# Normalised tiles transposed on TensorE instead of by DMA, with one PSUM bank set aside for it

## The chip, the cores and the metric

The kernel runs on one core of one Trainium2 chip. The metric is device time in microseconds (us) of one execution, all inputs in device memory at the start. The kernel before takes 1333.68 us (median of three runs, 1333.62 to 1335.79). In what follows PE is the matrix engine TensorE, PEld its weight loads, DVE is VectorE, ACT ScalarE, POOL GpSimd, and SP the engine that issues most of the DMAs. PSUM is the small memory that TensorE writes its results to, here eight banks of 128 x 512 fp32; SBUF is the large on-chip memory that everything else reads.

## What is computed

Two kinds of layer, each applied twice in turn to x (2048 positions, 1024 channels, bf16). Cut to what matters:

```
def _A_ref(x, wqkv, wo):          # attention, 32 heads of 32, window of 8 positions, 2 apart
    q, k, v = split(x @ wqkv)
    idx = pos[:, None] - arange(8)[None, :] * 2      # masked where negative
    attn = softmax(einsum("bhsd,bhswd->bhsw", q, k[idx]) * scale)
    return einsum("bhsw,bhswd->bhsd", attn, v[idx]) @ wo

def _B_ref(x, w1, b1, w2, b2):    # MLP over positions: S=2048 -> F=3584 -> S=2048
    u = gelu(einsum("bsd,sf->bdf", layernorm(x), w1) + b1)
    return (einsum("bdf,fs->bds", u, w2) + b2).transpose

x = x + A(layernorm(x));  x = x + B(layernorm(x))
x = x + A(layernorm(x));  x = x + B(layernorm(x))
```

## The kernel before

**Tiling.** Positions are taken in two classes, even (c = 0) and odd (c = 1), since the attention window steps by two; each class is 8 tiles of 128 positions by 1024 channels. A layer pair (`li` = 0, 1) is attention, then the MLP.

**hT.** The projections of attention need the normalised input with channels on the partitions, so each 128 x 1024 tile must be transposed after its layer norm. `hT[c][hf]` holds a class in two halves of 512 positions (four tiles each). For the first class of the first layer `first_tiles` does this on TensorE (`turn`, L278 to L281: eight 128 x 128 transposes into a PSUM bank; `place`, L284: one copy to hT). All the others, 24 tiles, go through `to_hT` (L231, L232): one transposing DMA from SP's queue. They are

- the second class of layer 0, normalised in `prologue_tile` (L334): 8 tiles early in the kernel; odd tiles are normalised on ACT, even ones on DVE;
- the first class of layer 1: `gemm2_tile` (L638) computes a tile of the MLP's second product (56 matmuls into two banks), adds bias and residual on DVE (L654), normalises into `hb` (DVE), and hands it to `to_hT`: 8 tiles one after another between the layers;
- the second class of layer 1, again `gemm2_tile`, normalised on ACT for six of eight tiles: 8 tiles, mixed into attention as fill.

**Attention.** `project` (L389) takes one output tile and one half: 8 matmuls (L400) into one bank, copied by ACT to q, k or v (L404, L407). `qk` (L422) multiplies q and shifted k on DVE (T, L430) and sums over channels on TensorE (L435). Softmax runs on DVE and ACT, its result goes to device memory and comes back spread over partitions (`pb`, L472); `pv` multiplies and adds on DVE (L490, L501, L503). `out_proj` (L560, matmuls L590) closes the layer. `gemm1` (L613, matmuls L623) is the first product of the MLP.

**Order.** `weave` (L685) walks the steps of attention (the lead) and, where its own running estimate of TensorE and DVE time says that the next TensorE step would wait, pulls a unit of fill: in this order second-class tiles, v projections of the second class (`v_ahead`), and, once `out0` is opened, output projection of the first class and partial sums of the MLP. In that estimate the step that ends a tile of the second class counts 0.6 us of TensorE time. This sets the order in which the instructions are traced. The order on each engine is then fixed when the program is built, by priorities in order of tracing; only the opening (`first_tiles`) is pinned by hand on PE, DVE, ACT and POOL. `proj_pair` (L410) has a special order for the pair that opens a class: k and q of the first half of the positions, then of the second half, so that the first 32 matmuls need only tiles 0 to 3. For c = 0 it serves layer 1 alone, since layer 0 opens with `first_tiles`.

**Queues and banks.** SP's queue carries every weight load (L378 wq and wv, L567 wo, L610 w1, L677 w2) and, between them, the transposing DMAs of L232; POOL's queue carries activations (xs, xr, xa, xb) and the softmax traffic. PSUM: the pool `psp` has 6 banks, shared by everything that TensorE accumulates, and `pssp` holds the scores in 2.

Of the kernel before, what the change touches and what calls it, by code (L numbers as in the profile page):

```python
# [13 lines left out]
BF16 = mybir.dt.bfloat16  # L14

P = 128
# [10 lines left out]
def kernel(  # L27
# [13 lines left out]
    nc = tc.nc  # L41
# [4 lines left out]
    KD = D // P  # L46
# [24 lines left out]
    def pool(name, bufs, **kw):  # L71
        return ctx.enter_context(tc.tile_pool(name=name, bufs=bufs, **kw))
# [9 lines left out]
    pbp = pool("pbp", 2)  # L82
    otp = pool("otp", KD)
    dram = pool("dram", 1, space=bass.MemoryType.DRAM)
    psp = pool("psp", 6, space=bass.MemoryType.PSUM)
    pssp = pool("pssp", 1, space=bass.MemoryType.PSUM)

    class at:
# [15 lines left out]
    def bank(name="ps"):  # L104
        return psp.tile([P, 512], FP32, name=name, tag="ps")

    def x2(name, shape=None, dt=BF16):
        return x2p.tile(shape or [P, D], dt, name=name, tag="x2")
# [14 lines left out]
    ident = const.tile([P, P], BF16, name="ident")  # L123
# [70 lines left out]
    def stats_dve(x, mul, eps):  # L194

        s = st("bn", [P, D // 512, 6])
        for cc in range(D // 512):
            nc.vector.bn_stats(out=s[:, cc, :], in_=x[:, cc * 512:(cc + 1) * 512])
        mv = st("mv", [P, 2])
        nc.vector.bn_aggr(out=mv[:], in_=s[:])  # L200
        rs = st("rs", [P, 1])
        rsqrt(rs[:], mv[:, 1:2], mul, eps)
        return mv[:, 0:1], rs

    def stats_act(x, mul, eps, junk, sums=None):

        s1 = sums
        if s1 is None:
            s1 = st("s1", [P, NDC])
            for n in range(NDC):  # L210
                nc.scalar.activation(out=junk[:, n * 512:(n + 1) * 512], in_=x[:, n * 512:(n + 1) * 512],
                                     func=ACT.Identity, accum_out=s1[:, n:n + 1])
        t1 = st("t1", [P, 1])
        nm = st("nm", [P, 1])
        nc.scalar.activation(out=t1[:], in_=s1[:, 1:2], func=ACT.Copy, scale=-1.0 / D)
        nc.scalar.activation(out=nm[:], in_=s1[:, 0:1], func=ACT.Identity, bias=t1[:], scale=-1.0 / D)
        ss = st("ss", [P, 1])
        nc.scalar.activation(out=junk, in_=x, func=ACT.Square, bias=nm[:], accum_out=ss[:])  # L218
        rs = st("rs", [P, 1])
        rsqrt(rs[:], ss[:], mul / D, eps)  # L220
        return nm, rs

    def norm_dve(dst, x, mean, rs, op=ALU.subtract):
        nc.vector.tensor_scalar(out=dst, in0=x, scalar1=mean, scalar2=rs[:], op0=op, op1=ALU.mult)

    def norm_act(dst, x, nm, rs):
        bi = st("bi", [P, 1])
        nc.scalar.activation(out=bi[:], in_=nm[:], func=ACT.Identity, scale=rs[:])
        nc.scalar.activation(out=dst, in_=x, func=ACT.Identity, bias=bi[:], scale=rs[:])  # L229

    def to_hT(h, hT, c, i):  # L231
        nc.sync.dma_start_transpose(out=hT[c][i // 4][:, :, (i % 4) * P:(i % 4 + 1) * P], in_=h)  # L232

    def staged(c, i):
        n = (i + c * (NT - 1)) % NT
# [98 lines left out]
    def prologue_tile(c, i, hT):  # L334
        t = staged(c, i)
        if i % 2:
            junk = x2("junk")
            nm, rs = stats_act(t, 1.0, eps1, junk[:])
            norm_act(t, t, nm, rs)
        else:  # L340
            mean, rs = stats_dve(t, 1.0, eps1)
            norm_dve(t, t, mean, rs)
        to_hT(t, hT, c, i)
# [5 lines left out]
    class Attn:  # L349
# [58 lines left out]
                               in_=ps[:].unsqueeze(1).to_broadcast([P, 2, HT]))  # L408

        def proj_pair(self, c, pair, parts):  # L410
            if pair == 0 and 0 in parts:
                for hf in range(2):
                    for part in parts:
                        for dt in range(2):
                            yield from self.proj(c, part, dt, hf)
                return
            for part in parts:
                for hf in range(2):
                    for dt in (2 * pair, 2 * pair + 1):
                        yield from self.proj(c, part, dt, hf)  # L420
# [217 lines left out]
    def gemm2_tile(c, i, w2t, src, dst, hT, on_act=False, end=False):  # L638
        xs = x2("xs")
        nc.gpsimd.dma_start(out=xs[:], in_=src[c][i * P:(i + 1) * P, :])  # L640
        xo = x2("xo")
        halves = [slice(n * 512, (n + 1) * 512) for n in range(NDC)]
        groups = [halves[:1], [slice(512, 768)], [slice(768, 1024)]] if end else [halves]
        for cols in groups:
            acc = [bank() for _ in cols]
            for n in range(NW2):
                for ft in range(n * HF, (n + 1) * HF):
                    for ps, xc in zip(acc, cols):
                        nc.tensor.matmul(ps[:, 0:xc.stop - xc.start], lhsT=w2t[n][:, ft % HF, c::DIL],  # L649
                                         rhs=g[ft // GF][:, ft % GF, xc], start=(ft == 0), stop=(ft == FT - 1))  # L650
                if n < NW2 - 1:
                    yield 1.5 * len(cols), 0.0
            for ps, xc in zip(acc, cols):
                nc.vector.scalar_tensor_tensor(out=xo[:, xc], in0=ps[:, 0:xc.stop - xc.start], scalar=b2_sb[:, i, c:c + 1],  # L654
                                               in1=xs[:, xc], op0=ALU.add, op1=ALU.add)
            yield 1.5 * len(cols), 0.75 * len(cols)
            if end:
                nc.sync.dma_start(out=dst[:, cols[0]], in_=xo[:, cols[0]])
        if not end:
            nc.gpsimd.dma_start(out=dst, in_=xo[:])  # L660
        if hT is None:
            return
        hb = x2("hb")
        if on_act:
            nm, rs = stats_act(xo[:], 1.0, eps1, hb[:])
            norm_act(hb[:], xo[:], nm, rs)
        else:
            mean, rs = stats_dve(xo[:], 1.0, eps1)
            norm_dve(hb[:], xo[:], mean, rs)
        to_hT(hb[:], hT, c, i)  # L670
        yield 0.6, 0.0 if on_act else 2.0

    def w2_tiles(i):
# [72 lines left out]
    hT = [[None, None] for _ in range(DIL)]  # L746
    new_hT(hT, 0)
    for li in range(2):
# [15 lines left out]
        def second_class():  # L764
            new_hT(hT, 1)
            for i in range(NT):
                if first:
                    prologue_tile(1, i, hT)
                    yield 0.6, 2.0 * (i % 2 == 0)
                else:  # L770
                    yield from gemm2_tile(1, i, w2_tiles(i), xa[0], xb[1][i * P:(i + 1) * P, :], hT, on_act=i < NT - 2)
# [20 lines left out]
        if first:  # L792
            with at(top):
                ln_exp_table()
            hT = [[None, None] for _ in range(DIL)]
            new_hT(hT, 0)
            for i in range(NT):
                run(gemm2_tile(0, i, w2_tiles(i), xa[0], xb[0][i * P:(i + 1) * P, :], hT))
        else:
            for i in range(NT):  # L800
                w2t = w2_tiles(i)
                for c in range(DIL):
                    run(gemm2_tile(c, i, w2t, xa[1], out_v[c, i], None, end=(i == NT - 1 and c == DIL - 1)))
# [30 lines left out]
```

## Time and profile before

| what | value |
|---|---|
| median of three runs | 1333.68 us |
| the profiled execution, its own time | 1335.79 us |
| its span, first to last instruction | 1334.0 us |
| granted TensorE clock, mean | 0.992 |
| PE busy, first product of the MLP (L623) | 386.2 us |
| PE busy, second product of the MLP (L649) | 388.6 us |
| transposing DMAs (L232) | 24, landing 3.0 / 4.1 / 12.3 us after issue (min / median / max) |
| 256-byte packets (those of the transposes) in the DMA record | 24,576, 6.29 MB |

How to read it: busy is the time in which an engine had an instruction running. A matmul of 512 columns is shown as 379 ns long, but the next one starts 216 ns after it: 56 matmuls of a `gemm2_tile` take 12.1 us. Idle time that the profile lists before an instruction is followed by what ended it ("<-DMA w" is a weight load that landed). SP is shown by what it issues: the start of a line is the moment at which SP got to that DMA, after waiting for its data or its buffer, and everything behind it in the queue waits too.

The stretches of the kernel: 0 to 33 us opening; 33 to about 260 attention of layer 0 with fill; to 490 the rest of the output projection and the MLP's first product; 488 to 585 the eight `gemm2_tile`s of the first class; 585 to about 910 attention of layer 1, into which the second class's eight are mixed (up to 777); then the MLP of layer 1 to the end.

### The profile page before, as it was taken

Reading aid. Unit: us, or ns where it says so; the run is one execution under the profiler, and the core shown is the slowest. Engines: PE = TensorE matmul, PEld = TensorE weight load, DVE = VectorE, ACT = ScalarE, POOL = GpSimd, SP = SyncE. Lnnn points to the kernel's source line nnn. Section 1 sums busy time; section 2 is a strip of 40 time slices with the busy share of each in tenths; the row PEclk is TensorE's granted clock in tenths of the full one; section 3 lists DMA queues with packets and bytes.
Section 4 is the critical chain, followed back from the end, with each engine's and each line's share of the span. In section 5 each row is a group of like instructions: output and inputs, shape, how many; then the busy total and the mean of one; then the engine's idle time right before and its main releaser. Section 6 shows DMA issues by size and latency. Waiting matters only on the chain. (4 is left out here: it accounts for less than half of the span.)

```text
span 1334.0 us, 15448 instructions
## 1 busy us (share of the span) xinstructions
PE 1285.8 (96%) x6226; PEld 582.9 (44%) x6348; DVE 658.4 (49%) x785; ACT 456.8 (34%) x808; POOL 95.5 (7%) x230
## 2 busy tenths in 40 slices
PE   8997999998999999999999999999999999999999
PEld 5343443343444444444444444444444444444444
DVE  6669597969401322325693149957981033110111
ACT  6844445931222430022524425477313234000000
POOL 3000001100100000000001110011020000000000
PEclk9998999998999999999999999999999999999999
DMA  9652525462522238873748962616444232334331
GB/s 258 138 134 63 135 81 144 159 162 71 173 63 79 77 105 222 212 179 90 179 118 219 252 163 64 157 65 179 129 123 122 63 95 71 117 89 142 117 115 61
DMA packets 239448, 173.00 MB, mean 130 GB/s; under 512 B 32208, under 2 KB 227152, under 8 KB 237328
## 3 DMA queue, kind: packets, MB, share of 16 engines
q1 hardware_dynamic: 224432, 116.67, 32.8%
q0 software_dynamic: 14368, 54.29, 14.7%
q8 instruction: 49, 0.80, 0.2%
q10 hardware_dynamic: 576, 1.05, 0.2%
q14 instruction: 23, 0.19, 0.0%
HBM read 146.81 MB, written 18.87 MB: 124 GB/s over the span
## 5 line engine op out<-in xcount | busy, mean ns | idle before, releaser
L649 PE MATMUL ps<-g,w 128*128 128x512 bf16 (+1 forms) x1781 | 388.6, 377 | 6.9 <-DMA w<-in_B_w_dram 4.8
L623 PE MATMUL ps<-h,w 128*128 128x512 bf16 x1757 | 386.2, 379 | 4.4 <-ACT h L229 2.3
L649 PEld LDWEIGHTS <-w 128*128 128x128 bf16 x1820 | 177.7, 98 | 217.3 <-DMA w<-in_B_w_dram 5.8
L623 PEld LDWEIGHTS <-w 128*128 128x128 bf16 x1792 | 175.3, 98 | 214.6 <-issue 3.6
L400 PE MATMUL ps<-hT,wq 128*128 128x512 bf16 (+1 forms) x1150 | 257.5, 376 | 5.2 <-issue 2.5
L654 DVE SCALAR_TENSOR_TENSOR xo<-ps,b_sb,xs 128x512 bf16<-128x512 f32 (+1 forms) x65 | 45.6, 738 | 296.7 <-PE ps L649 265.2
L430 DVE TENSOR_TENSOR T<-q,k 128x4096 bf16<-128x4096 bf16 x64 | 143.2, 2285 | 72.8 <-ACT q L404 52.7
L400 PEld LDWEIGHTS <-wq 128*128 128x128 bf16 x1176 | 114.4, 100 | 142.6 <-issue 17.5
L634 DVE TENSOR_TENSOR tmp<-ps,g 128x512 f32<-128x512 f32 x80 | 55.3, 692 | 213.6 <-PE ps L623 209.4
L501 DVE TENSOR_TENSOR pr<-pr 128x2048 bf16<-128x2048 bf16 x120 | 112.9, 947 | 0.6
L590 PE MATMUL ps<-wo,oT 128*128 128x512 bf16 x373 | 94.4, 383 | 8.6 <-DVE oT L503 6.8
L407 ACT CAST k<-ps 128x1024 bf16<-128x1024 f32 x64 | 64.6, 1014 | 86.9 <-PE ps L400 74.8
L490 DVE TENSOR_TENSOR pr<-pb,g 128x2048 bf16<-128x2048 bf16 x64 | 77.0, 1217 | 27.5 <-DMA pb<-pd 26.1
L400 PE MATMUL ps<-hT,wv 128*128 128x512 bf16 x376 | 87.6, 384 | 0.6 <-issue 0.2
L635 ACT ACTIVATE g<-tmp,b_sb 128x512 bf16<-128x512 f32 x80 | 57.7, 721 | 82.1 <-DVE tmp L634 82.1
L490 DVE TENSOR_TENSOR pr<-pb,v 128x2048 bf16<-128x2048 bf16 x64 | 76.3, 1215 | 10.7 <-DMA pb<-pd 9.8
L629 ACT CAST g<-ps 128x512 bf16<-128x512 f32 x80 | 45.7, 587 | 69.5 <-PE ps L623 69.2
L191 ACT ACTIVATE ln<-mv,eps 128x1 f32<-128x1 f32 x37 | 10.9, 294 | 166.7 <-DVE mv L200 159.5
L590 PEld LDWEIGHTS <-oT 128*128 128x128 bf16 x384 | 37.5, 99 | 56.3 <-DVE oT L503 7.8
L400 PEld LDWEIGHTS <-wv 128*128 128x128 bf16 x384 | 42.7, 114 | 43.1 <-issue 7.0
L435 PE MATMUL sc<-T,sel 128*32 128x512 bf16 x512 | 38.9, 387 | 15.2 <-DVE T L430 14.9
L404 ACT CAST q<-ps 128x512 bf16<-128x512 f32 x64 | 37.0, 584 | 48.0 <-PE ps L400 47.7
(97 smaller groups left out, 643.3 us busy)
## 6 DMA issues: line engine op xcount, KB each, us to landing
w<-in_B_w_dram SPq DMA_DIRECT2D x96, 448.0 KB, 3.8
w<-in_B_w_dram SPq DMA_DIRECT2D x56, 512.0 KB, 4.9
wq<-in_A_wqkv_dram SPq DMA_DIRECT2D x40, 512.0 KB, 4.3
pb<-pd POOLq DMA_DIRECT2D x16, 1024.0 KB, 10.7
wo<-in_A_wo_dram SPq DMA_DIRECT2D x16, 512.0 KB, 3.9
xa<-xn POOLq DMA_DIRECT2D x32, 256.0 KB, 3.2
xs<-xa POOLq DMA_DIRECT2D x32, 256.0 KB, 3.5
wv<-in_A_wqkv_dram SPq DMA_DIRECT2D x12, 512.0 KB, 5.0
```

The costliest lines, as they stand in the source:

```text
L400: nc.tensor.matmul(ps[:, lo:hi], lhsT=cols, rhs=self.hT[c][hf][:, kt, lo:hi], start=(kt == 0), stop=(kt == KD - 1))
L407: nc.scalar.copy(out=window(buf, 0, PADK + hf * HT, [(KW + 1, 2), (1, HT)]), in_=ps[:].unsqueeze(1).to_broadcast([P, 2, HT]))
L430: nc.vector.tensor_tensor(out=T[:], in0=q[:].unsqueeze(1).to_broadcast([P, 4, SC]), in1=window(k, par, 2, [(2, 4), (1, SC)]), op=ALU.mult)
L490: nc.vector.tensor_tensor(out=pr[:, :, u, :], in0=pb[:, :, u, :], in1=window(v, par, 2 + hf * HT, [(TB, 4), (2, 4), (1, TB)]), op=ALU.mult)
L501: nc.vector.tensor_tensor(out=pr[:, :, 0:wd, :], in0=pr[:, :, 0:wd, :], in1=pr[:, :, wd:2 * wd, :], op=ALU.add)
L590: nc.tensor.matmul(ps[:], lhsT=at_.oT[c][kt][:, i * P:(i + 1) * P], rhs=wo_t[n][kt // 4][:, kt % 4, :], start=(kt == 0), stop=(kt == KD - ...
L623: nc.tensor.matmul(ps[:], lhsT=wt[c][:, i, fl * P:(fl + 1) * P], rhs=h2[c][i // 4][:, i % 4, dc * 512:(dc + 1) * 512], start=(k == 0), sto ...
L629: nc.scalar.copy(out=gs, in_=ps[:])
L634: nc.vector.tensor_tensor(out=tmp[:], in0=ps[:], in1=gs, op=ALU.add)
L635: nc.scalar.activation(out=gs, in_=tmp[:], func=ACT.Gelu_apprx_tanh, bias=b1_sb[:, ft:ft + 1])
L649: nc.tensor.matmul(ps[:, 0:xc.stop - xc.start], lhsT=w2t[n][:, ft % HF, c::DIL], rhs=g[ft // GF][:, ft % GF, xc], start=(ft == 0), stop=(f ...
L654: nc.vector.scalar_tensor_tensor(out=xo[:, xc], in0=ps[:, 0:xc.stop - xc.start], scalar=b2_sb[:, i, c:c + 1], in1=xs[:, xc], op0=ALU.add, ...
```

## The change

`to_hT` no longer issues a DMA. It transposes the tile on TensorE, eight 128 x 128 transposes into a bank of a new pool `pstp` (one buffer), and copies the bank to hT. All its callers leave `on_dve` at False, so all 24 copies are made by ACT. The shared pool `psp` shrinks from 6 banks to 5. In `proj_pair` the half-by-half order is kept for the second class and dropped for the first, so layer 1 now traces k of both halves, then q of both halves. `weave`, its costs, `gemm2_tile`'s matmuls and the w2 loads are not touched.

```diff
-    psp = pool("psp", 6, space=bass.MemoryType.PSUM)
+    psp = pool("psp", 5, space=bass.MemoryType.PSUM)
+    pstp = pool("pstp", 1, space=bass.MemoryType.PSUM)
...
-    def to_hT(h, hT, c, i):
-        nc.sync.dma_start_transpose(out=hT[c][i // 4][:, :, (i % 4) * P:(i % 4 + 1) * P], in_=h)
+    def to_hT(h, hT, c, i, on_dve=False):
+        tp = pstp.tile([P, KD, P], BF16, name="tp", tag="tp")
+        for kt in range(KD):
+            nc.tensor.transpose(tp[:, kt, :], h[:, kt * P:(kt + 1) * P], ident[:])
+        dst = hT[c][i // 4][:, :, (i % 4) * P:(i % 4 + 1) * P]
+        if on_dve:
+            nc.vector.tensor_copy(out=dst, in_=tp[:])
+        else:
+            nc.scalar.copy(out=dst, in_=tp[:])
...
         def proj_pair(self, c, pair, parts):
-            if pair == 0 and 0 in parts:
+            if c and pair == 0 and 0 in parts:
...
-        to_hT(hb[:], hT, c, i)
+        to_hT(hb, hT, c, i)
```

## The prediction

> **What bounds the kernel now.** I read the page's first part, then busy time stretch by stretch, then who waits for whom, on PE and in SP's queue.
>
> ```profile
> PE 1285.8 (96%) x6226; PEld 582.9 (44%) x6348; DVE 658.4 (49%) x785; ACT 456.8 (34%) x808; POOL 95.5 (7%) x230
> ...
> 33.00:66.00 33.00, 29.86 (x171) 11.87 (x173) 21.62 (x17) 27.57 (x62) 1.07 (x2) 0.95 0.65 143
> 100.00:120.00 20.00, 12.45 (x65) 5.25 (x65) 19.09 (x17) 5.26 (x6) 0.00 (x0) 0.83 0.17 53
> 490.00:585.00 95.00, 94.53 (x433) 43.09 (x441) 24.01 (x43) 4.31 (x15) 7.50 (x14) 1.00 0.83 212
> 700.00:740.00 40.00, 35.01 (x153) 15.70 (x155) 11.62 (x15) 17.94 (x39) 4.96 (x9) 0.96 0.92 231
> ```
>
> The columns of a stretch are its length, then busy time and instructions of PE, PEld, DVE, ACT, POOL, then clock, DMA share, GB/s. PE is busy 96% of the span: whatever is added to PE lengthens the kernel, except where PE idles. It idles 48 us in all (1334.0 - 1285.8), hardly at all between the layers (490 to 585), but 7.5 us in 100 to 120, where DVE is full, and 5 us in 700 to 740, where DMA is. In 33 to 66 ACT is the fullest engine but PE.
>
> ```profile
> PE sc L435 <- DVE T L430: 14.9, 13, 4.6
> PE ps L590 <- DVE oT L503: 6.8, 2, 4.3
> PE ps L649 <- DMA w<-in_B_w_dram: 4.8, 2, 3.0
> ...
> 715.75 9.46 SPq L232 DMA_TRANSPOSE hT<-hb  x1
> 725.31 0.53 SPq L677 DMA_DIRECT2D w<-in_B_w_dram  x1
> 730.54 1.23 SPq L232 DMA_TRANSPOSE hT<-hb  x1
> 731.87 1.80 SPq L677 DMA_DIRECT2D w<-in_B_w_dram  x3
> ```
>
> The first three lines say what PE waits for (total, times, longest). The others say why weights were late: a transposing DMA held SP's queue for 9.46 us, and the next waited for its tile to be normalised, with w2 loads behind both. PE's two waits for w, 1.78 and 3.05 us, end when those loads land.
>
> **Step 1, the transposes on PE.** The opening already does this operation.
>
> ```profile
> 12.84 0.61 PE L281 MATMUL tp<-ident,g 128*128 128x128 bf16 x8
> 13.28 1.04 PE L400 MATMUL ps<-hT,wq 128*128 128x256 bf16 x8
> 14.16 0.61 PE L281 MATMUL tp<-ident,g 128*128 128x128 bf16 x8
> 14.60 2.00 PE L400 MATMUL ps<-hT,wq 128*128 128x256 bf16 x16
> ```
>
> From the start of eight transposes to the next matmul it is 0.44 us (13.28 - 12.84, 14.60 - 14.16), elsewhere in the opening 0.46; I take 0.45. So 24 tiles add 24 x 0.45 = 10.8 us of PE work, 3.6 us for each group of eight tiles.
>
> The Trainium skill ("VectorE: DVE Perf Modes", "Rules for kernel authors") advises TensorE for a 128 x 128 transpose where a PSUM destination will do, and its table gives 390 ns by TensorE against 1309 ns by DMA. That advice compares one transpose with another, while the rows above have PE as the full engine and the transposing DMAs off it. With the page's 390 ns for each of 192 transposes the added PE work would be an estimated 75 us, against the row's 10.8.
>
> Between the layers nothing hides the 3.6 us (PE busy 94.53 of 95): the whole is paid. In attention of layer 1 PE is also the bound while the second class is mixed in: 3.6 us paid, less step 4. In layer 0 the eight tiles come at 34 to 60 us, and PE later waits 4.57 and 2.77 us for T (at 106 and 111), so 3.6 us fit into idle that exists, as long as the DVE chain ahead of T isn't late. That depends on step 2.
>
> **Step 2, the copies on ACT.**
>
> ```profile
> L284 ACT COPY hT<-tp 128x1024 bf16<-128x1024 bf16 x2 | 2.0, 993 | 0.0
> ```
>
> 24 x 0.99 = 23.8 us of ACT. Between the layers ACT is idle (4.31 of 95) and in attention of layer 1 about a third busy: free there. In layer 0 it isn't: ACT has almost no gap from 28.7 to 60, with the stats of the odd tiles and the k and q copies, and DVE's next T starts at 56.07 after waiting 1.14 us for such a q copy. Eight copies, 7.9 us, go into that stretch; those traced ahead of the q copies delay T, softmax, and the T for which PE waits at 106. Bounds: 0 (all fall behind the q copies) and 7.9 (all ahead). By the planner's own costs four of the eight tiles are traced ahead, 4.0 us, and some of that fits between; I take 2.0 for layer 0, its PE work being covered by the idle at 106 and 111. If that cover is gone, 3.6 more.
>
> **Step 3, PE waiting for the tile.** The transposes need hb, so they cannot follow the tile's last matmul at once.
>
> ```profile
> 500.06 1.41 DVE L654 SCALAR_TENSOR_TENSOR xo<-ps,b_sb,xs 128x512 bf16<-128x512 f32 x2 [11.29 <-PE ps L649]
> 503.50 0.55 DVE L224 TENSOR_SCALAR hb<-xo,mv,rs 128x1024 bf16<-128x1024 bf16 x1 [0.60 <-ACT rs L192]
> ...
> 598.98 1.46 PE L649 MATMUL ps<-g,w 128*128 128x512 bf16 x6
> 600.42 0.62 PE L435 MATMUL sc<-T,sel 128*32 128x512 bf16 x8
> 600.97 1.69 PE L649 MATMUL ps<-g,w 128*128 128x512 bf16 x7
> ```
>
> hb is ready 3.99 us after the accumulation ends (503.50 + 0.55 - 500.06); with the normalisation on ACT 6.2 us (724.35 to 730.51). If PE's order were the traced one, it would stand idle that long. The last three lines speak against it: the score matmuls, traced earlier, sit inside one 14-matmul piece of a fill tile, right where T ends. So PE's order is set by estimated readiness, and the transposes should land inside the next tile's matmuls. How well is readiness estimated? At 602.62, 604.82 and 607.02 the score matmuls start 0.12 to 0.14 us later than the matmuls ahead of them would let them. I take 0.15 us for each of 16 tiles, 2.4 us. Bounds: 0, and the whole chain (a rival below). A late PE makes nothing else late but the copy, whose reader comes a class later.
>
> **Step 4, what the DMAs' going gives back.** L232 leaves SP's queue. The waits in attention of layer 1 that end on a load behind it are 1.78 and 3.05 us (w2) and 1.2 us (wq, at 660); the openings of the two classes wait 0.51 (591.6) and 1.1 us (784) for the last tile's landing. 7.7 us in all is the most; 0 the least, since 700 to 740 is also full of softmax traffic (DMA share 0.92; transposes' 256-byte packets are 57 of 586 us there). I take 4.5: the two w2 waits, nearly whole. DMA time itself is nowhere else on the path.
>
> **Step 5, five banks.** A group of eight matmuls fills a bank in 1.73 us; one bank fewer lets PE run one group less ahead of a late reader. Least 0; most one such group at each of PE's four longest waits for DVE (4.57, 4.3, 2.77, 2.5 us), 6.9 us. I take one, 1.7.
>
> The Trainium skill ("Perfetto Trace Analysis", "Matmuls") wants independent groups rotated through different PSUM banks so that evacuation overlaps the next group. No wait in this trace names a bank, so the page alone would add nothing that the bound above lacks.
>
> **Step 6, the order of the first pair in layer 1.** Before, 32 matmuls (7.07 us from 584.50) need only tiles 0 to 3. Traced k first, 16 do (3.46 us), to 588.0; the last tile's hb comes at 588.5, transposes and copy take it to about 590.3. If q's first half is pulled forward, 0; if not, 2.3 us. I take 0.5, since order follows readiness.
>
> **Sum:** 3.6 + 3.6 (PE work) + 2.0 (layer 0) + 2.4 (late hb) - 4.5 (SP) + 1.7 (banks) + 0.5 (order) = +9.3 us. The profiled execution took 1335.79 us (span 1334.0, 1.8 around it), so it would become 1345.1; it stands 2.1 above the median 1333.68, so the median forecast is **1343.0 us**, 0.7% slower. The likeliest case's own range is 1337 to 1352.
>
> **Rivals.**
> - **Queue relief wins (faster).** All 7.7 us of step 4 come back, layer 0 costs nothing, and the spread loads pb, for which DVE waits 36.0 us in total, land sooner without the transposes: if 5 us of that reach PE (it waits 21.7 us for DVE in the two lines above), 7.2 - 7.7 - 5 = -5.5, 1328. It decides if PE's waits for w vanish and those for T shrink by over 4 us. Against it: the early pb waits (84 to 95 us) have no transposes beside them. Chance 0.11.
> - **Gains and costs cancel.** 7.2 + 2.4 - 7.7 = +1.9, 1335.6, if layer 0, banks and order are free. Chance 0.16.
> - **Readiness misjudged.** The DVE-ACT-DVE chain is harder to estimate than one T: about 1.2 us per tile instead of 0.15 gives 16 x 1.05 = 17 more, 1360. For it: two engines hand over four times. Chance 0.13.
> - **Traced order holds on PE.** 10 tiles at 3.99 and 6 at 6.2 us are 77 us in place of 2.4: 1418. Against it: the split groups. Chance 0.04.
> - **The change isn't what its words say.** They speak of fill only where attention blocks and of w2 tiles used for both halves; `weave` and the w2 loops are untouched in the diff, so nothing is booked for them.
>
> **Numbers.** The forecast has 0.56. A measurement of this kernel tells about 0.2% (2.7 us) from no change, so the edges are 1331.0 and 1336.4. Faster: 0.12 (the first rival, and a little of the second). Same: 0.13 (most of the second). Slower: 0.75. The range that should hold 8 in 10 leaves out the faster rival below and half of the misjudged case with the blocked one above: 1333 to 1357.
>
> **What would show it.** Eight transposes should stand inside the L649 stretches about 4 us after a tile's end, with under 0.3 us idle before them; the 490 to 585 stretch should lengthen by 4 to 5 us; the waits for w at 725 and 733 should go; T after the first pair of layer 0 should start 0 to 4 us later than 56.07. I am wrong if PE idles over 1 us before most transposes, if attention of layer 1 gets shorter by more than the 5 us of w waits, or if the first 120 us grow by over 8 us.

## The result, and the profile after

The changed kernel takes **1357.37 us** (median of four runs, 1354.6 to 1359.3) against 1334.74 for the kernel before on the same chip: ratio 1.0163, 95% interval 1.0136 to 1.0191, 1.6% slower. The forecast was 1343.0 with a range up to 1357: the direction was right, the time lies just above the range, and the loss, 22.6 us, is about two and a half times the 9.3 that were forecast. The profiled execution took 1357.69 us, its span is 1355.9, 21.9 more than the 1334.0 of before.

First the share of busy time by engine, on the page of after.

```profile
PE 1299.3 (96%) x6415; PEld 593.0 (44%) x6540; DVE 658.4 (49%) x785; ACT 480.3 (35%) x832; POOL 95.5 (7%) x230
```

PE is busy 13.5 us longer (1299.3 - 1285.8) where the forecast had 10.8 us of work; the two need not agree, since busy time counts eight transposes at 0.62 us, although the next matmul starts after 0.46, and counts matmuls at a lowered clock with their longer time. The span grew by 21.9, so 8.4 us of it are idle time that was not there. The same stretches as before, same columns (length, then busy time and instructions of PE, PEld, DVE, ACT, POOL, clock, DMA share, GB/s), tell where to look.

```profile
33.00:66.00 33.00, 29.12 (x203) 13.62 (x205) 21.22 (x17) 31.12 (x66) 1.08 (x2) 1.00 0.29 82
100.00:120.00 20.00, 15.90 (x83) 7.10 (x82) 19.64 (x18) 7.11 (x7) 0.00 (x0) 0.91 0.26 79
490.00:585.00 95.00, 92.94 (x462) 42.95 (x469) 23.50 (x42) 10.57 (x21) 7.50 (x14) 1.00 0.61 181
700.00:740.00 40.00, 29.09 (x136) 13.78 (x137) 14.08 (x20) 15.28 (x31) 4.42 (x8) 0.87 0.74 188
```

Between the layers (490 to 585) PE idles 2.1 us where it idled 0.5. In 700 to 740 it idles 10.9 where it idled 5.0, and the granted clock there is 0.87 instead of 0.96. Set against each other at points up to which PE has done the same work in both kernels, but for the transposes, the two profiled executions part like this (start of the instruction named, in us):

| point on PE | before | after | gained or lost since the point above |
|---|---|---|---|
| scores of the second pair, layer 0 | 58.41 | 59.82 | +1.4 |
| start of the MLP's second product | 487.81 | 484.48 | -4.7 |
| first scores of layer 1 | 600.42 | 604.65 | +7.6 |
| a later group of scores, layer 1 | 682.8 | 685.7 | -1.3 |
| first scores of the second class, layer 1 | 793.67 | 807.41 | +10.8 |
| a group of scores near the end of attention | 897.5 | 916.3 | +5.1 |
| end of the span | 1334.0 | 1355.9 | +3.1 |

What PE waits for (total us, times, longest):

```profile
PE tp L235 <- ACT hb L230: 12.0, 5, 10.2
PE sc L443 <- DVE T L438: 10.4, 12, 2.0
PE ps L598 <- DVE oT L511: 5.6, 2, 3.2
PE ps L598 <- DMA wo<-in_A_wo_dram: 3.5, 1, 3.5
PE ps L631 <- ACT h L230: 2.4, 2, 1.9
PE tp L235 <- DVE hb L225: 2.3, 9, 0.4
PE ps L631 <- DVE xn L604: 2.2, 1, 2.2
...
PE ps L408 <- ACT hT L240: 1.1, 1, 1.1
```

The line for w2 (4.8 us before) is gone, as forecast. In its place stand two lines for the transposes, 12.0 and 2.3 us, of which one wait alone is 10.2. The wait for wo grew from 1.3 to 3.5, and one for `xn` is new. The long wait in the timeline of all engines (start, length, engine, line and what it does, then the idle time before it and what ended it):

```profile
705.33 0.63 POOL L466 DMA_DIRECT2D pd<-Pb  x1 [54.94 <-DVE Pb L463]
...
710.73 0.51 POOL L480 DMA_DIRECT2D pb<-pd  x1 [4.77 <-issue]
...
713.00 0.52 POOL L480 DMA_DIRECT2D pb<-pd  x1 [1.76 <-issue]
...
714.41 0.57 POOL L648 DMA_DIRECT2D xs<-xa  x1
...
717.49 5.99 PE L657 MATMUL ps<-g,w 128*128 128x512 bf16 x27
...
727.45 1.41 DVE L662 SCALAR_TENSOR_TENSOR xo<-ps,b_sb,xs 128x512 bf16<-128x512 f32 x2 [15.69 <-DMA xs<-xa]
...
732.37 1.24 ACT L230 ACTIVATE hb<-xo,bi,rs 128x1024 bf16<-128x1024 bf16 x1
733.66 1.03 PE L235 MATMUL tp<-ident,hb 128*128 128x128 bf16 x8 [10.18 <-ACT hb L230]
```

Read from the bottom: PE stops at 723.48 (717.49 + 5.99) and stands 10.18 us before eight transposes, because `hb` of that tile is ready only at 733.6. `hb` is late because DVE waited 15.69 us for `xs`, the residual. `xs` is late because its load is the last in POOL's queue behind the store of the softmax result, which had waited 54.94 us for its data, and two loads of pb. The wait was there before the change, as the same place in the kernel before shows:

```profile
724.35 1.41 DVE L654 SCALAR_TENSOR_TENSOR xo<-ps,b_sb,xs 128x512 bf16<-128x512 f32 x2 [15.52 <-DMA xs<-xa]
...
727.17 6.22 PE L649 MATMUL ps<-g,w 128*128 128x512 bf16 x27 [1.78 <-DMA w<-in_B_w_dram]
...
736.43 3.73 PE L649 MATMUL ps<-g,w 128*128 128x512 bf16 x10 [3.05 <-DMA w<-in_B_w_dram]
```

There the tile's transposing DMA stood in SP's queue until 730.54 with w2 loads behind it, and PE went on with other matmuls, but for waits of 1.78 and 3.05 us for those loads; now the tile holds PE itself.

The clock tells what comes on top (windows of after, same columns as above):

```profile
733.40:737.40 4.00, 3.52 (x14) 1.90 (x16) 0.00 (x0) 1.22 (x2) 0.54 (x1) 0.50 0.26 63
...
882.00:886.00 4.00, 3.70 (x15) 0.91 (x15) 1.05 (x2) 1.27 (x5) 0.38 (x1) 0.50 0.04 10
```

After the 10.2 us wait, and again after the 3.5 us wait for wo, PE runs at half speed: from its new start at 733.66 and at 882.30 to where the clock's record goes back to full, 738.1 and 888.2, some 2.2 and 2.9 us lost. Four matmuls after the wo wait take 1.87 us, the same four before the change 1.02:

```profile
866.33 1.02 PE L590 MATMUL ps<-wo,oT 128*128 128x512 bf16 x4 [1.28 <-DMA wo<-in_A_wo_dram]
```

```profile
882.30 1.87 PE L598 MATMUL ps<-wo,oT 128*128 128x512 bf16 x4 [3.50 <-DMA wo<-in_A_wo_dram]
```

The kernel before has one such stretch in layer 1 (735.9 to 739.3, with its 3.05 us wait for w2, which ends at 736.43), worth some 1.4. The Trainium skill ("TensorE: Matmul & The Clock Gate", Part 1) says that an idle window of about 3.4 us puts TensorE at half rate for a window; waits of 3.05, 3.5 and 10.2 us were followed by 0.5 here, and the first of them is shorter than the page's window.

### The profile page after: what moved, and what is told of

Read it like the earlier page. It is cut to its first block, busy times and chain, and to the rows that moved or that the text cites. A ratio compares the mean times of both kernels' runs of the same rounds, so it can differ in the third digit from the quotient of the medians.

```text
span 1355.9 us, 15783 instructions
## 1 busy us (share of the span) xinstructions
PE 1299.3 (96%) x6415; PEld 593.0 (44%) x6540; DVE 658.4 (49%) x785; ACT 480.3 (35%) x832; POOL 95.5 (7%) x230
## 5 line engine op out<-in xcount | busy, mean ns | idle before, releaser
L408 PEld LDWEIGHTS <-wq 128*128 128x128 bf16 x1176 | 114.6, 100 | 137.3 <-issue 14.9
L192 ACT ACTIVATE ln<-mv,eps 128x1 f32<-128x1 f32 x37 | 10.9, 294 | 158.4 <-DVE mv L201 151.1
L639 ACT ACTIVATE g<-ps,b_sb 128x512 bf16<-128x512 f32 x32 | 22.0, 687 | 83.2 <-PE ps L631 77.7
```

The costliest lines, as they stand in the source:

```text
L408: nc.tensor.matmul(ps[:, lo:hi], lhsT=cols, rhs=self.hT[c][hf][:, kt, lo:hi], start=(kt == 0), stop=(kt == KD - 1))
```

## The experiments

Eleven kernels. Ratios are to the kernel before on the same chip, with 95% intervals.

**1. Five banks alone** (`bank5`, from the kernel before).

```diff
-    psp = pool("psp", 6, space=bass.MemoryType.PSUM)
+    psp = pool("psp", 5, space=bass.MemoryType.PSUM)
```

> The kernel before with the shared PSUM pool at 5 banks instead of 6 (the sixth stays empty), nothing else. Theory A (the loss is PE standing in front of transposes whose tile is late; banks are not on the path): 1331 to 1337 us, waits of PE for T and for oT within 2 us of before. Theory B (the lost bank carries a good part of the 22 us, above all the late waits of PE at 878, 985 and 1020 us of the changed kernel): 1339 to 1345, and those waits appear here too. Prediction's step 5 had +1.7, at most +6.9.

1335.93 against 1335.74: ratio 1.0011 (0.9995 to 1.0028), span 1333.7. The bank costs nothing that can be told. One wait changes its name:

```profile
PE ps L649 <- DVE xo L654: 2.8, 1, 2.8
...
PE ps L649 <- DMA w<-in_B_w_dram: 0.6, 1, 0.6
```

With five banks PE stops for a bank that `xo` has not been read out of (late through the same `xs`); with six it ran on and stopped for w2. The stop moved, and the time did not grow: the two lines make 3.4 us, against 4.8 for w2 before.

**2. The change for one group of eight tiles at a time.** All three have the new pool, five banks and the new `proj_pair`; `to_hT` gets a flag, and the groups without it keep the DMA.

```diff
+    def to_hT(h, hT, c, i, on_dve=False, on_pe=True):
+        if not on_pe:
+            nc.sync.dma_start_transpose(out=hT[c][i // 4][:, :, (i % 4) * P:(i % 4 + 1) * P], in_=h[:])
+            return
...
-        to_hT(t, hT, c, i)                       # prologue_tile
+        to_hT(t, hT, c, i, on_pe=False)          # between_pe, second_pe
...
-        to_hT(hb[:], hT, c, i)                   # gemm2_tile
+        to_hT(hb, hT, c, i, on_pe=False)         # prologue_pe
+        to_hT(hb, hT, c, i, on_pe=c == 0)        # between_pe
+        to_hT(hb, hT, c, i, on_pe=c == 1)        # second_pe
```

`prologue_pe`, the second class of layer 0 alone:

> The changed kernel, but only the eight second-class tiles of layer 0 are transposed on PE; the 16 tiles of the MLP's second product go by DMA as before (5 + 1 banks, new order of the first pair). Theory A: the first 485 us as in the changed kernel, 3.3 us shorter than before, and the rest as before: 1329 to 1333. Theory B (banks): the late waits stay, 1335 to 1341. Prediction's step 2 had +2.0 for this part.

1344.16, ratio 1.0069 (1.0043 to 1.0095). The scores of the second pair came 3.2 us late, as step 2 has it, and at the start of the MLP's second product nothing of it was left (-0.7 against before): the idle time near 106 to 118 swallowed it. The loss is elsewhere, at the opening of layer 1, where nothing is transposed on PE: without the half-by-half order 16 matmuls are ready there, and then PE waits 4.0 us for the DMA of the last tile (+6.3 in all). The order of the first pair and the DMA do not go together, and the expectation had missed that.

`between_pe`, the first class of layer 1 alone:

> The changed kernel, but only the eight first-class tiles of layer 1 (between the layers) are transposed on PE; the 16 of the second class, in both layers, go by DMA. Theory A: 8 x 0.45 us of transposes, some 0.3 us of wait before each, 1.3 us at the opening: +6 to +8, 1339 to 1342, with 0.2 to 0.6 us idle before each group of transposes and none above 1.5. Theory C (the long stall needs only PE transposes anywhere): a stall near 10 us at about 725.

1343.66, ratio 1.0071 (1.0041 to 1.0101), a little above the 1339 to 1342 expected. First scores of layer 1 are 7.6 us later, reckoned from the start of the second product, exactly as in the whole change; after them nothing more is lost up to 860. No wait before the transposes is longer than 0.42 us.

`second_pe`, the second class of layer 1 alone:

> The changed kernel, but only the eight second-class tiles of layer 1 (mixed into attention) are transposed on PE; the 16 others go by DMA. Theory A: one stall of 9 to 11 us near 720 to 735 in front of the transposes of the third tile, since its residual xs lands late; 8 x (0.45 + 0.5) us more; the waits for w2 (4.8 us) and for wq (1.2) gone: +8 to +15, 1342 to 1349. Theory B (banks): under +5 from this part. Prediction's steps 1, 3 and 4 had 3.6 + 1.2 - 4.5 = +0.3 for it.

1355.26, ratio 1.0143 (1.0111 to 1.0176), above the 1342 to 1349 expected. Here are both the long wait and, under "issue", the one that `prologue_pe` shows at the opening, which the expectation had again left out:

```profile
PE tp L238 <- ACT hb L230: 13.0, 5, 10.9
PE ps L411 <- issue: 4.7, 6, 3.8
PE ps L601 <- DVE oT L514: 4.3, 2, 2.4
PE ps L601 <- DMA wo<-in_A_wo_dram: 3.8, 1, 3.8
PE ps L634 <- DVE xn L607: 2.5, 1, 2.5
```

So the largest part of the loss comes with the second class, inside attention. The wait for `xn` appears with this group alone; the wait for wo is longer than the 1.3 us of before in all three kernels (3.0, 2.7, 3.8), and experiment 6 takes it up. The three spans do not add up to the whole (7.6 + 6.8 + 21.3 against 21.9), since two of them pay for the order of the first pair a price that the whole change does not.

**3. Is it the late `xs`?** `xs_sp` is the change with one more edit: for these eight tiles `xs` is loaded from SP's queue instead of POOL's. The number of instructions on PE, DVE and ACT is the same.

```diff
-        nc.gpsimd.dma_start(out=xs[:], in_=src[c][i * P:(i + 1) * P, :])
+        xs_eng = nc.sync if c == 1 and hT is not None else nc.gpsimd
+        xs_eng.dma_start(out=xs[:], in_=src[c][i * P:(i + 1) * P, :])
```

> The changed kernel with one edit: the second class's residual tile xs (layer 1) is loaded from SP's queue instead of POOL's, where it stands behind the softmax store pd (which waits some 55 us for DVE) and the two 1 MB loads of pb. Theory A (the 10.2 us stall is: xs late, so xo late, so hb late, and PE stands in front of that tile's transposes): the stall falls below 2 us, and with it the half-speed clock after it (2.2 us): 1344 to 1348. Rival D (the normalisation on ACT is the late part): stall stays 8 to 11 us, 1354 to 1359. Rival E (DMA is simply full at 710 to 727): xs lands just as late from SP, stall over 5 us.

1350.01, ratio 1.0107 (1.0076 to 1.0138), 7.4 us below the change; span 1345.3, 10.6 below. From its timeline:

```profile
710.36 0.55 SPq L649 DMA_DIRECT2D xs<-xa  x1
...
715.56 1.41 DVE L663 SCALAR_TENSOR_TENSOR xo<-ps,b_sb,xs 128x512 bf16<-128x512 f32 x2 [2.03 <-DMA xs<-xa]
...
726.33 1.52 SPq L649 DMA_DIRECT2D xs<-xa  x1
...
732.43 1.41 DVE L663 SCALAR_TENSOR_TENSOR xo<-ps,b_sb,xs 128x512 bf16<-128x512 f32 x2 [15.46 <-DMA xs<-xa]
...
738.64 0.92 PE L235 MATMUL tp<-ident,hb 128*128 128x128 bf16 x8 [2.89 <-ACT hb L230]
```

DVE's 15.69 us wait for that tile's `xs` is now 2.03, and PE's wait for the tile 0.31 (at 725.42) instead of 10.18; the half-speed stretch behind it is gone (granted clock 0.99 in 700 to 740). From issue to use the load took 5.2 us through SP's queue (710.36 to 715.56), against 13.0 through POOL's behind the pb loads (714.41 to 727.45). The tile before it costs PE 1.53, and the next one's `xs`, issued from SP at 726.33 behind w2 loads, is late in its turn, for 2.89; after that wait the clock is at 0.5 again, from 738.8 to 742.2. The late `xs` is what the 10 us are made of. The expected 1344 to 1348 was not quite reached in the median: the waits before the other transposes, and for wo and `xn`, are still there.

The same edit in the kernel before (`before_xs_sp`):

> The kernel before with the same xs edit. Theory A: tile 2 of the second class is normalised in time, its transposing DMA no longer holds SP's queue, the w2 loads behind it land in time, PE's two waits for w (1.8 and 3.0 us) and the half-speed clock after them (1.7 us) go: 1328 to 1332, faster than both. Rival E (DMA full): both waits stay within 1 us, 1333 to 1337.

**1330.84, ratio 0.9975 (0.9955 to 0.9994)**, the lowest median of this study and inside the 1328 to 1332 expected. PE's wait for w2 falls from 4.8 to 1.5 us, and from 683 to the first scores of the second class it gains 5.0 us of span. SP's waits for an `hb` normalised on ACT, with the weight loads behind them, fell from 13.6 to 7.4 us in all.

**4. The order of the first pair** (`half`: the change, with the half-by-half order back for both classes).

```diff
-            if c and pair == 0 and 0 in parts:
+            if pair == 0 and 0 in parts:
```

> The changed kernel with the half-by-half order of the first pair put back. Theory A: the wait of 1.1 us for the copy at 592 and part of the 0.4 us before the transposes go: -1.0 to -1.6, 1355 to 1357, everything else as in the changed kernel, with the long stall and the late waits for wo (near 878) and xn (near 1020) again. Rival: if those two late waits were chance of one execution, they are absent or much shorter here, and the time is 1349 to 1353.

1354.14, ratio 1.0132 (1.0106 to 1.0158), a little more gain than expected; its span is 2.2 us below the change. The opening of layer 1 shows both orders, the change first and then this kernel:

```profile
587.11 3.62 PE L408 MATMUL ps<-hT,wq 128*128 128x512 bf16 x16
591.14 0.62 PE L235 MATMUL tp<-ident,hb 128*128 128x128 bf16 x8 [0.42 <-DVE hb L225]
592.86 10.52 PE L408 MATMUL ps<-hT,wq 128*128 128x512 bf16 x47 [1.10 <-ACT hT L240]
```

```profile
588.00 4.05 PE L408 MATMUL ps<-hT,wq 128*128 128x512 bf16 x18
592.03 0.62 PE L235 MATMUL tp<-ident,hb 128*128 128x128 bf16 x8
592.49 9.88 PE L408 MATMUL ps<-hT,wq 128*128 128x512 bf16 x45
```

In the change PE does 16 matmuls, then waits 0.42 us for the tile and 1.10 for the copy; q's first half, whose data were there, was not pulled forward. With the half order both waits are gone. The waits of 9.6 us for `hb`, 3.2 for wo and 2.3 for `xn` come back here, so they are no accident of one execution.

**5. What lets the transposes float at all** (`share6`: the change with the transposes in the shared pool of six banks).

```diff
-        tp = pstp.tile([P, KD, P], BF16, name="tp", tag="tp")
+        tp = psp.tile([P, KD, P], BF16, name="tp", tag="ps")
```

> The changed kernel, but the transposes take their bank from the shared pool, put back to 6 banks, and there is no pool of their own. The build then leaves every group of transposes right behind its tile's 56 matmuls. Theory A: PE stands for the whole chain at each of the 16 tiles of the MLP's second product: 10 x 4 us and 6 x 6 us, plus the late xs: 1385 to 1425. Rival (PE hides it by pulling matmuls ahead on the chip): within 5 us of the changed kernel.

1455.82 (one run), span 1454.0, 9% slower and above the 1385 to 1425 expected.

```profile
PE tp L234 <- ACT hb L229: 45.9, 5, 21.7
PE tp L234 <- DVE hb L224: 38.9, 10, 4.0
...
495.68 5.78 PE L656 MATMUL ps<-g,w 128*128 128x512 bf16 x26
505.50 1.03 PE L234 MATMUL tp<-ident,hb 128*128 128x128 bf16 x8 [4.05 <-DVE hb L224]
506.33 14.34 PE L656 MATMUL ps<-g,w 128*128 128x512 bf16 x56
```

The first two lines are waits (total, times, longest), the others the timeline. PE waits for the whole chain before the transposes: 3.9 to 4.05 us for a tile normalised on DVE, some 6.1 for one on ACT, 21.65 for the one with the late `xs`, 84.8 us in all against 14.3 in the change. After such a wait the clock is lowered too: 56 matmuls in one piece run at a granted clock of 0.85 (14.34 us instead of 12.1), which neither the expectation nor the rival "traced order holds on PE" had reckoned with; the rival's 4 and 6 us a tile are right. As far as these two builds show, groups that share a PSUM pool stand on PE in traced order, and groups from a pool of their own (scores, and in the change the transposes) are placed where they are reckoned to be ready. Experiment 4 fits this: k's and q's groups share a pool.

**6. Why wo is late, and by how much the place of a code load matters.** In the trace the chip fetches code in packets of 16 KB on a queue of its own (on the page of before, the queue "q8 instruction" has 49 packets, 0.80 MB), some 0.9 to 1.6 us on one DMA engine each. Late in attention of layer 1 (852.48 before, 866.91 after) two pb loads are issued, with a wo load near them; one code packet falls at a different place after the first pb issue:

| kernel | code packet, us after that pb issue | PE waits for wo |
|---|---|---|
| before, bank5, before_xs_sp | 14.9, 15.2, 14.9 | 1.3, 1.6, 1.5 |
| after, half, xs_sp | 4.3, 4.6, 5.8 | 3.5, 3.2, 2.7 |
| prologue_pe, between_pe, second_pe | 3.4, 1.2, 2.7 | 3.0, 2.7, 3.8 |
| share6, and xs_defer of experiment 7 | 9.0, 6.8 | 3.4, 2.7 |

The change makes PE's program 384 instructions longer. Supposing that a packet holds 256 instructions of PE, this shifts the packets by half of one. Two kernels test it on the kernel before, by longer or shorter rows of tiny matmuls in the opening's warm-up, of about the same total length: 128 more PE instructions (`pad128`) and 256 more (`pad256`).

```diff
+            if n == 16:
+                for _ in range(80):              # pad256: 144, and 56 columns
+                    nc.tensor.matmul(ps[:, 0:96], lhsT=ident[:], rhs=ident[:, 0:96], start=True, stop=True)
+                return
```

> The kernel before with 64 more tiny matmuls in the warm-up of its opening (80 of 96 columns for 16 of 512, about the same PE time): 128 more PE instructions, nothing else. Theory F (the late wait for wo near 860 to 880 is a code load: a 16 KB instruction fetch falls into the 1 MB loads of pb once PE's program is 128 instructions longer, modulo 256): the fetch stands 1 to 6 us after pb's issue, pb lands 1 us later, PE waits 2.5 to 4 us for wo instead of 1.3: +1 to +3, 1335 to 1339. Rival G (the PE transposes or the banks do it): wo waits 1.3 to 1.8 us as before, 1333 to 1336.

> The same with 128 more tiny matmuls (144 of 56 columns): 256 more PE instructions, one whole 16 KB block, so that by theory F the fetch stands where it stood before (about 15 us after pb's issue) and PE waits 1.2 to 1.8 us for wo: 1333 to 1337. If any longer program lengthens the wait, it is 2.5 us or more here too.

`pad128` puts the packet 0.5 us after the pb issue, pb lands after 8.07 and 12.35 us instead of 7.06 and 11.18, wo after 6.99 instead of 4.87, and PE waits 3.4 us for it, then runs at half clock from 860.5 to 863.8: from 859 to 897 this kernel loses 3.8 us. `pad256` has the packet at 15.1 again, waits 2.1 (more than the 1.2 to 1.8 expected, less than the 2.5 of the rival) and loses 0.8. So the wait follows the place of the code load, and a kernel that adds instructions moves it without touching wo; the 0.8 us between `pad256` and before is not the packet's. But against the expectation the whole of `pad128` is not slower: 1332.3, ratio 0.9971 (0.9953 to 0.9989). In layer 0 it is 4.6 us ahead by 118 and 7.8 by 488. Another packet falls among the first two pb loads in the kernel before (at 90.6; they land 7.2 and 12.9 us after issue) and behind them in `pad128` (at 94.1, landing after 6.6 and 10.6); but `pad256`, with this packet among those loads again (at 88.8), is 4.1 ahead by 488, so the packet is at most a part of it. `pad256` took 1336.78, ratio 0.9998 (0.9978 to 1.0018).

**7. What is left without the waits** (`xs_defer`: the change, with `xs` from SP as in 3, the half order as in 4, and each tile's transposes traced three quarters into the next tile's matmuls).

```diff
+                if n == 2 and hT is not None and pending:
+                    pending.pop()()
...
-        to_hT(hb, hT, c, i)
+        pending.append(partial(to_hT, hb, hT, c, i))
+        if i == NT - 1:
+            pending.pop()()
```

> The changed kernel with three edits: xs of layer 1's second class from SP, the half-by-half order back, and each tile's transposes traced three quarters into the next tile's matmuls, so that hb has 9 us to come. Theory A: the 8.0 us that PE still waited for hb in the xs run fall below 1.5, and so does the wait at the opening: 1337 to 1342, what is left being 7 us of PE work for 16 tiles and the later wait for wo, less the w2 waits. Rival (the transposes' PE work costs more than 0.45 us a tile): above 1345.

1340.6, ratio 1.0023 (1.0009 to 1.0037), span 1339.5.

```profile
506.43 0.61 PE L235 MATMUL tp<-ident,hb 128*128 128x128 bf16 x8
506.88 12.25 PE L658 MATMUL ps<-g,w 128*128 128x512 bf16 x55
518.97 0.61 PE L235 MATMUL tp<-ident,hb 128*128 128x128 bf16 x8
...
718.77 0.62 PE L235 MATMUL tp<-ident,hb 128*128 128x128 bf16 x8 [1.35 <-ACT hb L230]
```

No idle time stands before the transposes but the 1.35 us of the last line, the start of eight to the next matmul is 0.45 us, and the opening of layer 1 is reached 3.1 us later than before, reckoned from the start of the second product, instead of 7.6. At the first scores of the second class (793.7) it has lost 2.6 us by the same reckoning, for 7.2 us of added PE work: the queues pay for most of it, though a wait for wq has grown to 2.46 us (1.22 before) with half clock from 663.6 to 667.0 behind it. The rest of the loss comes after that: 2.7 us for wo with a piece of lowered clock (+3.0), and 2.2 for `xn`. The fair comparison is still `before_xs_sp`, which has the better queue for `xs` and no transposes on PE: 1330.84. Mended as far as these runs could, the transposes on PE stay some 6 us dearer by the two ratios (1.0023 against 0.9975) and 10 by the two medians, which come from different chips; up to 3 of that stand with the wait for wo, which follows the code load.

## Why the forecast had the sign and not the size

The +21.9 us of the span, by the forecast's own steps:

- **Step 1, PE work: right.** 0.46 us from the start of a tile's transposes to the next matmul (500.78 to 501.24), 0.45 forecast. `xs_defer` shows the 3.6 us between the layers as 3.1, with the opening's old 0.5 us wait for a landing gone.
- **Step 2, layer 0: its mechanism right, its price wrong.** The scores came 1.4 us late at the second pair and 3.1 at the third, inside the bounds, and +2.0 was forecast to stay. It was all swallowed by PE's later waits, and after is 3.3 ahead at 488. The clock has a part in this: PE's waits for T at 111 and 114 shrank from 4.57 and 2.77 us to 1.83 and 2.05, and the clock's record has 0.5 in layer 0 for 17 us before (39.6 to 43.0, 111.3 to 118.1, 316.1 to 322.9) and for 6.8 after (113.4 to 116.8, 314.8 to 318.2), worth up to 5 us. But the 3.3 us aren't the change's to claim: kernels whose layer 0 differs in nothing but a bank or a few warm-up instructions lie between 0.7 and 7.8 ahead of that same execution there.
- **Step 3, late hb: the step that failed.** That the transposes land inside the next tile's matmuls came true; the wait before them did not. The forecast booked 16 x 0.15 = 2.4 us. Measured are 12.0 + 2.3 = 14.3 us of waits before the transposes, and 2.2 of half clock behind the longest. A usual tile was dearer than booked, but not by much: between the layers the listed waits are 0.2 to 0.4, and from one tile's transposes to the next it is 12.91 us, against 12.53 in `xs_defer`, where they wait for nothing, so 0.38 a tile instead of 0.15; taking these waits away as well as the order brought 4.5 of the 7.6 us there. What failed is that the chain was counted from the moment at which its inputs were there, in every tile. One tile's `xs` is 15 us late through POOL's queue, and the place of its transposes in PE's order, settled when the program is built, does not allow for that. The forecast had this tile in hand: its 6.2 us are measured from 724.35 on, and the line of 724.35 ends with the 15.52 us wait for `xs`, which was left out. Nor did the sum have a term for the clock, though the kernel before already shows 0.83 in 100 to 120, where PE waits for T. The rival "readiness misjudged" came near in time (1360) with the wrong shape: not 1.2 us in every tile but 10 in one.
- **Step 4, the freed queue: right, and too small.** Forecast 4.5. The waits for w2 (4.8) and wq (1.2) went away, and so did the two old waits at the openings (0.51 and 1.1): 7.6 of the 7.7 that the step had as its most, and the 1.4 of half clock behind w2 as well.
- **Step 5, five banks: booked +1.7, measured -0.4 of span,** nothing within the interval.
- **Step 6, the order of the first pair: booked +0.5, measured 1.7 at the opening and 2.2 in the span.** The forecast took it that order follows readiness; within one PSUM pool the runs show the traced one.
- **Not booked at all:** the wait for wo, +2.2, with 2.9 of half clock behind it, which follows the place of a code load (experiment 6); 2.2 for `xn` and 0.7 for oT near the end. The `xn` wait appears in every kernel that transposes the second class on PE in its own pool and hardly in the others; DVE there waits 5.89 us for a store of `xa` that was issued among five w1 loads. Whether it is the shifted time of these loads or something else wasn't tried and stays open.

Added up from the lists of waits and the clock, the terms come near the whole: PE work of layer 1 +7.2, layer 0 -3.3 with its own PE work, late `hb` +14.3 and +2.2 of clock, the queue -7.6 and -1.4 of clock, the wait for the copy at the opening +1.1, wo +2.2 and +2.9 of clock, `xn` +2.2, oT +0.7, in all +20.5 of the 21.9. The rest can lie in what the listed waits leave out: they start where the last matmul ends as shown, 0.16 us after the next one could have started (0.379 - 0.216).

`weave` still counts what it counted before. No run here changed that, so what it costs is open.

## What to carry to other kernels

Before work is moved from a queue to the engine that bounds the kernel, look in the trace at what its input waits for in the worst tile, not in a usual one: the wait of 15 us that cost PE some 5 us by way of SP's queue stopped PE itself for 10, and lowered its clock behind that too. Where such a wait shows in the trace, mend it first; here that small edit alone made the kernel before 0.25% faster, and with it and a later place for the transposes the change came within 0.23% of the kernel before. Below half a per cent, add a variant with some extra instructions before believing in a mechanism: with 128 more PE instructions in the warm-up a single wait moved by 2 us and a long stretch by 8.

## What the runs showed of the hardware

- **Half clock after waits of a few us.** Waits of 2.89, 3.05, 3.4, 3.5 and 10.2 us on PE were each followed by some 3 to 6 us at a granted clock of 0.5. In the clock's record of all these kernels a lowered stretch lasts 3.41 us or a whole multiple of it (3.4, 6.8, 10.2, once 23.9), but for those cut off by the end of the program. Two shorter waits close together had the same effect: 1.83 and 2.05 us, ending at 111.28 and 113.95 in the changed kernel, came with 0.5 from 113.4 to 116.8. The edge isn't sharp: after the 2.7 us wait of `xs_defer` the clock was lowered as well (mean 0.66 in 867 to 872), after the 2.7 of `xs_sp` it stayed at 1.00 (868 to 880).
- **Data loads landed later with a code load among them.** In `pad128` one 16 KB packet on one DMA engine came with 1.0 to 1.2 us more for two 1 MB loads and 2.1 more for the weight load behind them.
- **Order on PE.** Moving the transposes into the shared PSUM pool cost 98 us (1455.82, one run, against 1357.37): each group of eight stood right behind its tile's 56 matmuls.
